# Attention block and SwiGLU on one core: tiles 4 to 7 transposed by DMA, and phi rows placed behind the next third product

## The chip, the cores and the metric

The kernel runs on one core of one Trainium2 chip. The metric is device time in microseconds (us) of one execution; the time of a kernel is the median of its runs. A core has five engines with instruction streams of their own that meet only at semaphores: PE (TensorE, matrix products into PSUM), DVE (VectorE), ACT (ScalarE), POOL (GpSimd) and SP (SyncE, which here only issues DMAs). "PEld" in the profile is the loading of PE's stationary operand, which overlaps its products.

## What is computed

The input x has 2048 tokens of width 1024. Its layer-normalized form xn feeds a linear attention of 32 heads of width 32 and a SwiGLU feed-forward of width 3584; the output joins them.

```python
xn = _layernorm(x)                        # (x - mean) / sqrt(var + 1e-5)
qkv = xn @ wqkv                           # q, k, v of 32 heads
phi = lambda t: where(t > 0, t + 1, exp(t)) + 1e-6
kv = einsum("bhsd,bhse->bhde", phi(k), v) # sums over all tokens
z = einsum("bhsd->bhd", phi(k))
o = (phi(q) @ kv) / (phi(q) . z + 1e-6)
s = o @ wo
g = silu((silu(xn @ w_gate) * (xn @ w_up)) @ w_down)
return x + s * g
```

## The kernel before

Tokens are cut into 16 tiles of 128 and into 4 blocks of 512 (block b holds tiles 4b to 4b+3; TPB = 4 tiles to a block); two blocks make a "pass" p, and `xnT[p]` holds xn transposed (features on partitions) for pass p, which is what every product needs. The matrix products of the later parts use Strassen's scheme with seven block products instead of eight: a group has part_a (products M3 and M4), part_b (M1, then M5 and M2) and part_c (N7 and N6), and each product needs sums of operand blocks that DVE forms. The stages, in order:

1. **Front** (to about 140 us; lines 264 to 755). Tile by tile: statistics, 1/sqrt, normalization, transposition, and the K and V products of tiles 0 to 8 and 12 directly; K, V and Q of the rest by Strassen groups (`KVGroup`, `QGroup`).
2. **Attention output** (to about 220 us; lines 757 to 886): KVZ, the last Q groups, numerator and denominator (ND), o written to DRAM and transposed back by DMA, times wo.
3. **Feed-forward** (the rest, lines 894 to 1230): gate and up products, h to DRAM, down product, output.

The front is written in a fixed order: inside `tc.manual_schedule(engines=FRONT_ORDER | {ET.SP})` PE, DVE, ACT, POOL and SP each run their instructions in the order in which the program emits them. An instruction that waits holds up everything behind it on its engine; on SP this includes the DMAs behind it. The names that the change touches:

- `emit_stats(i)` (L335, L348): two statistics instructions and an aggregation on DVE for tile i.
- `emit_rstd(i)` (L367 to L378): 1/sqrt for the tiles of one entry of `GROUPS`, which share one tile of results; three small instructions on DVE, then three Newton rounds of four small instructions on POOL (for block 3 these run on DVE). Before, tiles 0 to 3 are each their own group, {4, 5} and {6, 7} are groups, and blocks 2 and 3.
- `emit_N(i)` (L383): DVE normalizes tile i into its slot in the buffer `ws_all`. Tiles 4 to 7 have slots of their own; block 2's four slots are the same bytes, block 3's are others.
- `emit_T(i)` (L409, L425, L426): eight 128x128 PE transposes of tile i into two PSUM tiles, one copied to `xnT` by DVE, the other by ACT. Used for tiles 0 to 7.
- `emit_xT_block(b)` (L429, L430): for blocks 2 and 3, SP writes the block's normalized rows to `xn_dram` (1 MB), waits for that write, and issues one DMA transpose from there into `xnT`.
- `emit_B(i, c)` (L446 and the evictions L186, L187, L464): product of tile i with column chunk c of wk (c = 0, 1) or wv (c = 2, 3), eight matmuls of 512 columns; ACT takes exp and relu of K (then `emit_phi`, L190 and L191 on DVE, turns them into phi) or copies V. `emit_B_mm` and `emit_B_out` are its two halves.
- `emit_C(i)` (L475): PE adds phi(k) times v of tile i to the sums kvz; it needs phi of tile i and both V copies.
- `load_x`, `load_wkv`, and the Q weights (L315, two DMAs of 1 MB): loads issued by SP ahead of the fixed order; the Q weights wait by a gate (L755) for the first product of tile 3.
- `later`, `put` and `fill(n)`: a queue of DVE work that is put between the products by hand. In its order: statistics of block 2, its 1/sqrt, statistics of block 3, norms of block 2 and its `emit_xT_block`, 1/sqrt and norms of block 3 and its `emit_xT_block`, then the operand sums: `xs` of pass 0 (L138; the first of five reads block 0, the second block 1), sums of Q weights (L152 to L155), `xs` of pass 1 (the first reads block 2, the others block 3 too), and sums of K and V weights (L501 to L504).
- At the end of the front, `seq` runs eleven Strassen groups. Each iteration does part_a of a group, then part_c of the group before and its `post()` (for a Q or a K group two phi rows on DVE, four instructions), then its own part_b (whose first product is added to `qu` by DVE, L241 or L551), and then the C of tiles that have both phi(k) and v.

Of the kernel before, what the change touches and what calls it, by code (L numbers as in the profile page):

```python
# [21 lines left out]
def kernel(  # L22
# [11 lines left out]
    nc = tc.nc  # L34
    P = 128
# [12 lines left out]
    TPB = TB // P  # L48
# [215 lines left out]
    with ExitStack() as p1:  # L264
# [47 lines left out]
            load_wkv(c)  # L312
        for i in range(nx, NT):
            load_x(i)
        wq_loads = [nc.sync.dma_start(out=wq_sb[:, :, c * CW:(c + 1) * CW], in_=wqkv_v[:, :, c * CW:(c + 1) * CW])  # L315
                    for c in range(NCC)]

        SCH = min(nc.vector.BN_STATS_FMAX, D)
        NSC = D // SCH
# [3 lines left out]
        part_stats = {}  # L323


        GROUPS = [[t] for t in range(TPB)] + [[t, t + 1] for t in range(TPB, 2 * TPB, 2)]
        GROUPS += [list(range(b * TPB, (b + 1) * TPB)) for b in range(2, NB)]
        grp_of = {i: k for k, tiles in enumerate(GROUPS) for i in tiles}

        def emit_stats(i, parts=None):  # L330
            if i not in part_stats:
                part_stats[i] = small.tile([P, NSC, nc.vector.BN_STATS_DIM], FP32, name="stats", tag="stats")
            xr = x_ap(i).rearrange("p (c f) -> p c f", f=SCH)
            for c in (range(NSC) if parts is None else parts):
                nc.vector.bn_stats(out=part_stats[i][:, c, :], in_=xr[:, c, :])  # L335
            if parts is None:
                emit_aggr(i)
# [60 lines left out]
        def emit_N(i):  # L398
            emit_norm(i, xn_slot(i))

        def emit_T(i):

            h = DC // 2
            dst = xn_tok_ap(i)
            xn = xn_slot(i)

            def tr(t_ps, dcs):
                for k, dc in enumerate(dcs):
                    nc.tensor.transpose(t_ps[:, k, :], xn[:, dc * P:(dc + 1) * P], ident[:])  # L409

            if i == 0:
                tr_a = psB.tile([P, h, P], FP16, name="tr_ps", tag="B")[:]
                tr_b = psB.tile([P, h, P], FP16, name="tr_ps", tag="B")[:]
                emit_norm(i, xn[:, 0:h * P], cols=slice(0, h * P))
                tr(tr_a, range(0, h))
                emit_norm(i, xn[:, h * P:D], cols=slice(h * P, D))
                tr(tr_b, range(h, DC))
                nc.scalar.copy(out=dst[:, 0:h, :], in_=tr_a)  # L418
                nc.scalar.copy(out=dst[:, h:DC, :], in_=tr_b)
            else:  # L420
                tr_a = psB.tile([P, h, P], FP16, name="tr_ps", tag="B")
                tr_b = psB.tile([P, h, P], FP16, name="tr_ps", tag="B")
                tr(tr_a, range(0, h))
                tr(tr_b, range(h, DC))
                nc.vector.tensor_copy(out=dst[:, 0:h, :], in_=tr_a[:])  # L425
                nc.scalar.copy(out=dst[:, h:DC, :], in_=tr_b[:])  # L426

        def emit_xT_block(b):
            nc.sync.dma_start(out=blk_rows_pt(xn_dram, b), in_=xn_blk_slot(b))  # L429
# [22 lines left out]
        def emit_B_out(i, c):  # L452
            kv_ps = kv_tiles.pop((i, c))
            if c < NCC:
                if c == 0:
                    er_tiles[i] = exp_tile()
                    pk_tiles[i] = work.tile([P, D], BF16, name="pk_sb", tag="pk_sb")
                cs = slice(c * CW, (c + 1) * CW)
                emit_exp_relu(er_tiles[i][:, cs], pk_tiles[i][:, cs], kv_ps[:])
                if c == NCC - 1:  # L460
                    emit_phi(pk_tiles[i][:], er_tiles.pop(i)[:])
            else:
                vc = c - NCC
                nc.scalar.copy(out=v_of(i)[:, vc * GPC:(vc + 1) * GPC, 0:P],  # L464
                               in_=kv_ps[:].rearrange("p (g c) -> p g c", c=P))
# [126 lines left out]
        def fill(n):  # L592
            credit[0] += n
            while later and credit[0] > 0:
                weight, op = later.popleft()
                credit[0] -= weight
                op()
# [34 lines left out]
        with tc.manual_schedule(engines=FRONT_ORDER | {ET.SP}):  # L632

            warm_up(14)
            emit_stats(0, parts=(0,))
            emit_stats(0, parts=(1,))
            emit_aggr(0)
            emit_rstd_act(0)
            emit_T(0)
            emit_stats(1)  # L640
            warm_up(2)
            emit_B_mm(0, 0)
            emit_rstd_act(1)
            nc.scalar.preload_act_table(ACT.Exp)
            emit_N(1)
            emit_T(1)
            ln(2)
            emit_B_mm(1, 0)
            emit_B_out(0, 0)
            emit_B_mm(0, 1)  # L650
            emit_B_out(1, 0)
            emit_B_mm(1, 1)
            ln(3)
            emit_N(2)
            emit_B_out(0, 1)
            emit_B_mm(0, 2)
            emit_T(2)
            emit_B_out(1, 1)
            emit_B_mm(1, 2)
            emit_B_out(0, 2)  # L660
            emit_N(3)
            emit_B_mm(2, 0)
            emit_B_out(1, 2)
            emit_B_mm(2, 1)
            emit_stats(TPB)
            emit_T(3)
            emit_stats(TPB + 1)
            emit_rstd(TPB)
            emit_B_out(2, 0)
            emit_B_mm(2, 2)  # L670
            emit_B_out(2, 1)
            emit_stats(TPB + 2)
            emit_B_mm(0, 3)
            emit_B_out(2, 2)
            emit_B_mm(1, 3)
            emit_B_out(0, 3)
            emit_stats(TPB + 3)
            emit_rstd(TPB + 2)
            emit_C(0)
            emit_B_mm(2, 3)  # L680
            emit_B_out(1, 3)
            emit_N(TPB)
            emit_N(TPB + 1)
            emit_C(1)
            emit_B_mm(3, 0)
            emit_B_out(2, 3)
            emit_C(2)
            emit_B_out(3, 0)
            emit_B_mm(3, 1)
            fill(4)  # L690
            emit_T(TPB)
            emit_B_out(3, 1)
            emit_N(TPB + 2)
            emit_N(TPB + 3)
            emit_B_mm(3, 2)
            emit_T(TPB + 1)
            emit_B_out(3, 2)
            fill(2)
            emit_B(3, 3)
            fill(2)  # L700

            rest = list(range(TPB, 2 * TPB)) + [b * TPB for b in range(2, NB)]
            fills = {TPB: (3, 2, 2, 3), 2 * TPB: (5, 3, 2, 2), rest[-1]: (3, 4, 2, 2)}
            before = TPB - 1
            for i in rest:
                nf = fills.get(i, (3, 3, 2, 2))
                grp = QGroup(0, 0) if i == rest[-1] else None
                emit_B(i, 0)
                fill(nf[0])
                emit_C(before)  # L710
                before = i
                if grp:
                    grp.part_a()
                emit_B(i, 1)
                fill(nf[1])
                if grp:
                    grp.part_b()
                if i == TPB:
                    emit_T(TPB + 2)
                emit_B(i, 2)  # L720
                fill(nf[2])
                if i == TPB:
                    emit_T(TPB + 3)
                if grp:
                    grp.part_c()
                emit_B(i, 3)
                if grp:
                    grp.post()
                fill(nf[3])

            K, V = (lambda t: KVGroup(0, t)), (lambda t: KVGroup(1, t))
            Q = QGroup
            seq = [(lambda: Q(0, 1), 1, 0), (lambda: K(1), 1, 0), (lambda: Q(0, 2), 1, 1), (lambda: V(1), 2, 2),
                   (lambda: K(2), 0, 0), (lambda: V(2), 2, 1), (lambda: Q(0, 3), 0, 0), (lambda: K(3), 0, 0),
                   (lambda: Q(NPASS - 1, 0), 0, 0), (lambda: V(3), 0, 0), (lambda: Q(NPASS - 1, 1), 0, 0)]
            prev = None
            for make, fa, fb in seq:
                grp = make()
                grp.part_a()
                fill(fa)  # L740
                if prev:
                    prev.part_c()
                    prev.post()
                else:
                    emit_C(before)
                if make is not seq[-1][0]:
                    grp.part_b()
                    fill(fb)
                while ready_C:
                    emit_C(ready_C.popleft(), last=(not ready_C and make is seq[-1][0]))  # L750
                prev = grp
            qa = prev
            assert not later
        gate([x_loads[i] for i in range(first_wave, NT)], marks[("B", 1)], sync=True)
        gate(wq_loads, marks[("B", 3)], sync=True)  # L755

    with ExitStack() as p2:
        wop = p2.enter_context(tc.tile_pool(name="wop", bufs=1, reuse_waits="tile"))
# [502 lines left out]
```

## Time and profile before

| | |
|---|---|
| median of 3 runs | 752.52 us (751.88 to 752.78) |
| the profiled execution: time | 752.22 us |
| the profiled execution: span of its instructions | 750.4 us |
| granted TensorE clock | 1.00 throughout |
| PE transposes L409 | 64 (8 for each of tiles 0 to 7), from 6.5 to 45.8 us |
| DVE busy from 40 to 120 us | 18.4, 18.1, 17.2 and 17.4 of each 20 us |
| DMA engines idle | 26 to 32 us and 40 to 52 us |

A profile line in time order reads: start, duration, engine, line, operation, what it writes and reads, shape, count; in square brackets the idle time of the engine just before it and what ended that. "PEq", "SPq" and "ACTq" are the sequencers, SPq lines are DMA issues: the duration is how long SP is held by the issue, not how long the transfer takes. Where several alike instructions follow each other they are merged into one line with a count. Matmuls are pipelined and their printed ends are modelled, so two neighbours on PE overlap; the distance of their starts is what one costs.

### The profile page before, as it was taken

How to read it: one execution, taken by the hardware profiler on the slowest of the kernel's cores; microseconds unless marked ns; L12 is line 12 of the kernel's file. 1: busy time of each engine (PE TensorE's matmuls, PEld its weight loads, DVE VectorE, ACT ScalarE, POOL GpSimd, SP SyncE). 2: the span in 40 equal slices, each digit the busy share in tenths (PEclk: the TensorE clock that was granted, in tenths of full speed). 3: DMA queues.
4: the chain of work that ended last, by engine and by line, in shares of the span. 5: the costliest groups of instructions: out<-in, count | busy, mean ns of one | idle time of the engine just before them, and what ended most of it. 6: DMA issues, size and time to landing. Idle time of an engine off the chain costs nothing.

```text
span 750.4 us, 9920 instructions
## 1 busy us (share of the span) xinstructions
PE 741.2 (99%) x3700; PEld 350.0 (47%) x3740; DVE 510.0 (68%) x943; ACT 274.9 (37%) x482; POOL 51.6 (7%) x101
## 2 busy tenths in 40 slices
PE   9999999999999999999999999999999999999997
PEld 4554444454544444444444444444444444444454
DVE  6798977687754767886778767876755754445454
ACT  4444565655324434334343434333442111111111
POOL 3310000000000000000000000000000221121220
PEclk9999999999999999999999999999999999999999
DMA  9627000225689543665346633545879755554300
GB/s 317 219 81 169 1 1 0 71 81 130 191 235 301 151 111 99 197 183 145 105 130 179 207 113 93 173 148 150 275 242 332 297 183 183 182 183 160 106 29 29
DMA packets 127664, 115.99 MB, mean 155 GB/s; under 512 B 29440, under 2 KB 108416, under 8 KB 126336
## 3 DMA queue, kind: packets, MB, share of 16 engines
q1 hardware_dynamic: 122720, 106.58, 46.2%
q10 hardware_dynamic: 4896, 8.78, 3.4%
q8 instruction: 29, 0.48, 0.3%
q14 instruction: 19, 0.16, 0.1%
HBM read 70.52 MB, written 38.54 MB: 145 GB/s over the span
## 4 chain that ended last, share of the span: by engine, by line
PE 95%; DVE 2%; ACT 1%; issue 1%; DVEq 0%
PE X L131 29%; PE Y L131 29%; PE Z L131 10%; PE kv_ps L446 8%; PE s_ps L828 7%; PE qY L131 2%; PE qX L131 2%; PE kY L131 2%; PE kX L131 2%; PE nd_ps L791 1%; PE kvz L475 1%; PE w_ps L484 1%; PE qZ L131 1%; PE kZ L131 1%; PE tr_ps L409 0%
## 5 line engine op out<-in xcount | busy, mean ns | idle before, releaser
L131 PEld LDWEIGHTS <-ws_all 128*128 128x128 bf16 x1420 | 137.6, 98 | 162.1 <-issue 0.7
L924 DVE TENSOR_TENSOR q<-n,Y 128x512 f32<-128x512 f32 x63 | 43.3, 687 | 108.2 <-PE Y L131 105.1
L131 PEld LDWEIGHTS <-xs 128*128 128x128 bf16 (+1 forms) x736 | 69.6, 98 | 77.8 <-issue 1.4
L1194 POOL TENSOR_TENSOR o_out<-y,xres 128x512 bf16<-128x512 f32 x29 | 35.2, 1212 | 664.2 <-DVE y L1193 664.2
L131 PE MATMUL Y<-xs,ws_all 128*128 128x512 f16 (+3 forms) x308 | 70.3, 360 | 0.0
L131 PE MATMUL X<-xnT,ws_all 128*128 128x512 f16 (+1 forms) x278 | 70.1, 379 | 0.2
L131 PE MATMUL X<-xs,ws_all 128*128 128x512 f16 x224 | 57.5, 379 | 0.0
L131 PE MATMUL Z<-xs,ws_all 128*128 128x512 f16 x224 | 57.5, 379 | 0.0
L131 PE MATMUL Y<-xnT,ws_all 128*128 128x512 f16 x224 | 57.5, 379 | 0.0
L1048 ACT ACTIVATE g<-cg 128x512 bf16<-128x512 f32 x56 | 35.3, 630 | 54.1 <-DVE cg L939 54.1
L930 DVE TENSOR_TENSOR u<-Z,q 128x512 f32<-128x512 f32 x63 | 43.1, 685 | 16.0 <-PE Z L131 15.9
L1048 ACT ACTIVATE g<-X 128x512 bf16<-128x512 f32 x28 | 16.7, 597 | 99.5 <-PE X L131 99.5
L920 ACT COPY n<-X 128x512 f32<-128x512 f32 x63 | 36.9, 585 | 27.7 <-PE X L131 27.7
L446 PEld LDWEIGHTS <-xnT 128*128 128x128 f16 x320 | 30.5, 98 | 35.0 <-ACT xnT L418 0.5
L1073 DVE TENSOR_TENSOR ho<-g,up 128x1024 bf16<-128x1024 bf16 x56 | 38.1, 684 | 0.5
L446 PE MATMUL kv_ps<-wk_sb,xnT 128*128 128x512 bf16 x156 | 36.9, 379 | 0.5 <-DVE xnT L425 0.3
L1193 DVE TENSOR_TENSOR y<-y,s_in 128x512 f32<-128x512 f32 x31 | 22.2, 716 | 21.5 <-ACT y L1187 15.8
L446 PE MATMUL kv_ps<-wv_sb,xnT 128*128 128x512 bf16 x155 | 36.4, 379 | 0.2
L131 PEld LDWEIGHTS <-wg_sb 128*128 128x128 bf16 x224 | 21.9, 98 | 26.4
L131 PEld LDWEIGHTS <-wu_sb 128*128 128x128 bf16 x224 | 21.9, 98 | 26.4
L832 ACT CAST s_sb<-s_ps 128x512 bf16<-128x512 f32 x32 | 18.4, 584 | 37.9 <-PE s_ps L828 33.0
L1187 ACT ACTIVATE y<-X 128x512 f32<-128x512 f32 x8 | 4.8, 597 | 69.7 <-PE X L131 61.2
(179 smaller groups left out, 1140.6 us busy)
## 6 DMA issues: line engine op xcount, KB each, us to landing
h_dram<-ho SPq DMA_DIRECT2D x56, 256.0 KB, 2.6
wg_sb<-in_B_w_gate_dram SPq DMA_DIRECT2D x14, 512.0 KB, 4.0
wu_sb<-in_B_w_up_dram SPq DMA_DIRECT2D x14, 512.0 KB, 4.6
wdr<-in_B_w_down_dram SPq DMA_DIRECT2D x14, 512.0 KB, 4.3
ws_all<-h_dram SPq DMA_DIRECT2D x4, 1792.0 KB, 9.6
wds_dram<-wdsA SPq DMA_DIRECT2D x14, 384.0 KB, 2.8
hp_a<-h_dram SPq DMA_DIRECT2D x3, 1792.0 KB, 8.9
o_dram<-o_sb ACTq DMA_DIRECT2D x16, 256.0 KB, 2.9
```

What stands on the lines that cost most here:

```text
L131: marks["mm"] = nc.tensor.matmul(acc[:, 0:c1 - c0], lhsT=lhs(k), rhs=rhs(k)[:, c0:c1], start=(first and k == 0), stop=(k == n - 1), skip_g ...
L446: mm = nc.tensor.matmul(kv_ps[:], lhsT=xn_tok_ap(i)[:, dc, :], rhs=wkv_ap(c)[:, dc, :], start=(dc == 0), stop=(dc == DC - 1))
L475: nc.tensor.matmul(kvz_ps[j][:, gi, 0:P + 1], lhsT=pk_sb[:, g * P:(g + 1) * P], rhs=v_sb[:, g, 0:P + 1], start=(i == 0 and gi == 0), stop= ...
L828: mm = nc.tensor.matmul(s_ps[:], lhsT=oT[:, c, ttok], rhs=wo_sb[:, c, cc * CW:(cc + 1) * CW], start=(c == 0), stop=(c == G - 1))
L832: nc.scalar.copy(out=s_sb[:, cc * CW:(cc + 1) * CW], in_=s_ps[:])
L920: nc.scalar.copy(out=n[:], in_=self.X[:])
L924: nc.vector.tensor_tensor(out=self.q[:], in0=n[:], in1=self.Y[:], op=ALU.add)
L930: nc.vector.tensor_tensor(out=self.u[:], in0=Z[:], in1=self.q[:], op=ALU.add)
L1048: nc.scalar.activation(out=self.g[:, i, j * TB:(j + 1) * TB], in_=src, func=ACT.Silu)
L1073: nc.vector.tensor_tensor(out=self.ho[:, i], in0=self.g[:, i], in1=self.up[:, i], op=ALU.mult)
L1193: nc.vector.tensor_tensor(out=t[:], in0=t[:], in1=self.s_in[:, i, cs], op=ALU.mult)
L1194: (nc.vector if last and (i, j) != (0, 0) else nc.gpsimd).tensor_tensor(out=self.o_out[:, i, cs], in0=t[:], in1=self.xres[:, i, cs], op=AL ...
```

## The change

`GROUPS` becomes {0}, {1}, {2}, {3}, {4}, {5, 6, 7} and blocks 2 and 3. Tile 4's 1/sqrt is started right behind its statistics, ahead of the transposition of tile 3. `emit_T` isn't called for tiles 4 to 7 any more; in its place a new function, `emit_NT(i)`, normalizes a tile, writes its 256 KB of rows to `xn_dram` and transposes them by DMA into `xnT`, with both DMAs on SP and the second waiting for the first. Tile 4 goes there behind the phi of tile 2, tiles 5 to 7 together behind the product B(3,1). The two loads of the Q weights lose their gate and are issued by SP behind these, that is ahead of block 2's write. In the loop over `seq`, `post()` of the group before moves from ahead of part_b to behind it; the work of the `fill` after it stays behind both.

```diff
--- before.py
+++ after.py
@@ -312,8 +312,10 @@
             load_wkv(c)
         for i in range(nx, NT):
             load_x(i)
-        wq_loads = [nc.sync.dma_start(out=wq_sb[:, :, c * CW:(c + 1) * CW], in_=wqkv_v[:, :, c * CW:(c + 1) * CW])
-                    for c in range(NCC)]
+
+        def load_wq():
+            for c in range(NCC):
+                nc.sync.dma_start(out=wq_sb[:, :, c * CW:(c + 1) * CW], in_=wqkv_v[:, :, c * CW:(c + 1) * CW])
 
         SCH = min(nc.vector.BN_STATS_FMAX, D)
         NSC = D // SCH
@@ -323,7 +325,7 @@
         part_stats = {}
 
 
-        GROUPS = [[t] for t in range(TPB)] + [[t, t + 1] for t in range(TPB, 2 * TPB, 2)]
+        GROUPS = [[t] for t in range(TPB + 1)] + [list(range(TPB + 1, 2 * TPB))]
         GROUPS += [list(range(b * TPB, (b + 1) * TPB)) for b in range(2, NB)]
         grp_of = {i: k for k, tiles in enumerate(GROUPS) for i in tiles}
 
@@ -424,6 +426,13 @@
                 tr(tr_b, range(h, DC))
                 nc.vector.tensor_copy(out=dst[:, 0:h, :], in_=tr_a[:])
                 nc.scalar.copy(out=dst[:, h:DC, :], in_=tr_b[:])
+
+        def emit_NT(i):
+
+            emit_N(i)
+            rows = xn_dram[i * P:(i + 1) * P, :]
+            nc.sync.dma_start(out=rows, in_=xn_slot(i))
+            nc.sync.dma_start_transpose(out=xn_tok_ap(i), in_=rows)
 
         def emit_xT_block(b):
             nc.sync.dma_start(out=blk_rows_pt(xn_dram, b), in_=xn_blk_slot(b))
@@ -663,24 +672,23 @@
             emit_B_out(1, 2)
             emit_B_mm(2, 1)
             emit_stats(TPB)
+            emit_rstd(TPB)
             emit_T(3)
             emit_stats(TPB + 1)
-            emit_rstd(TPB)
             emit_B_out(2, 0)
             emit_B_mm(2, 2)
             emit_B_out(2, 1)
+            emit_NT(TPB)
             emit_stats(TPB + 2)
             emit_B_mm(0, 3)
             emit_B_out(2, 2)
             emit_B_mm(1, 3)
             emit_B_out(0, 3)
             emit_stats(TPB + 3)
-            emit_rstd(TPB + 2)
+            emit_rstd(TPB + 3)
             emit_C(0)
             emit_B_mm(2, 3)
             emit_B_out(1, 3)
-            emit_N(TPB)
-            emit_N(TPB + 1)
             emit_C(1)
             emit_B_mm(3, 0)
             emit_B_out(2, 3)
@@ -688,12 +696,11 @@
             emit_B_out(3, 0)
             emit_B_mm(3, 1)
             fill(4)
-            emit_T(TPB)
+            for i in range(TPB + 1, 2 * TPB):
+                emit_NT(i)
+            load_wq()
             emit_B_out(3, 1)
-            emit_N(TPB + 2)
-            emit_N(TPB + 3)
             emit_B_mm(3, 2)
-            emit_T(TPB + 1)
             emit_B_out(3, 2)
             fill(2)
             emit_B(3, 3)
@@ -715,12 +722,8 @@
                 fill(nf[1])
                 if grp:
                     grp.part_b()
-                if i == TPB:
-                    emit_T(TPB + 2)
                 emit_B(i, 2)
                 fill(nf[2])
-                if i == TPB:
-                    emit_T(TPB + 3)
                 if grp:
                     grp.part_c()
                 emit_B(i, 3)
@@ -740,19 +743,19 @@
                 fill(fa)
                 if prev:
                     prev.part_c()
-                    prev.post()
                 else:
                     emit_C(before)
                 if make is not seq[-1][0]:
                     grp.part_b()
-                    fill(fb)
+                if prev:
+                    prev.post()
+                fill(fb)
                 while ready_C:
                     emit_C(ready_C.popleft(), last=(not ready_C and make is seq[-1][0]))
                 prev = grp
             qa = prev
             assert not later
         gate([x_loads[i] for i in range(first_wave, NT)], marks[("B", 1)], sync=True)
-        gate(wq_loads, marks[("B", 3)], sync=True)
 
     with ExitStack() as p2:
         wop = p2.enter_context(tc.tile_pool(name="wop", bufs=1, reuse_waits="tile"))
```

## The prediction

> **What bounds the kernel now.** I read the engine table first, then PE's waits, then PE, DVE and the DMA queue of SP in order of time around the changed lines.
>
> ```profile
> PE 741.2 (99%) x3700; PEld 350.0 (47%) x3740; DVE 510.0 (68%) x943; ACT 274.9 (37%) x482; POOL 51.6 (7%) x101
> ```
> PE is busy for 741.2 of 750.4 us: only PE work removed, or one of its few stalls, can shorten the run. From 80 to 125 us its waits are these:
> ```profile
> PE kX L131 <- ACT v_sb L537: 0.6, 1, 0.6
> PE kvz L475 <- ACT v_sb L464: 0.3, 1, 0.3
> ```
> The PE timeline prices a PE transpose of a tile:
> ```profile
> 34.96 0.61 PE L409 MATMUL tr_ps<-ident,ws_all 128*128 128x128 f16 x8
> 35.41 1.67 PE L446 MATMUL kv_ps<-wv_sb,xnT 128*128 128x512 bf16 x7
> 37.13 0.61 PE L409 MATMUL tr_ps<-ident,ws_all 128*128 128x128 f16 x8
> 37.58 1.89 PE L446 MATMUL kv_ps<-wv_sb,xnT 128*128 128x512 bf16 x8
> ```
> The printed 0.61 overlaps what follows; start to start it is 0.45 us. A product of eight matmuls takes 1.73 us the same way.
>
> The DVE timeline after 70 us holds a second limit close under PE:
> ```profile
> 70.13 1.22 DVE L138 TENSOR_TENSOR xs<-xnT 128x2048 f16<-128x2048 f16 x1
> 72.56 3.50 DVE L138 TENSOR_TENSOR xs<-xnT 128x2048 f16<-128x2048 f16 x3 [1.22 <-DMA xnT<-xn_dram]
> ...
> 89.73 0.68 DVE L251 TENSOR_TENSOR pqT<-qu,qY 128x512 bf16<-128x512 f32 x1
> ```
> DVE waits 1.22 us for the transposed block 3 at 72.56, and then runs to L251 at 89.73 with no idle in brackets. L251 releases ACT (exp, relu, exp, relu, then the V copy L464), and PE waits for that copy:
> ```profile
> 92.84 0.39 PE L475 MATMUL kvz<-v_sb,pk_sb 128*128 128x129 bf16 x4 [0.27 <-ACT v_sb L464]
> ```
> So PE at 92.84 is tied to **block 3's landing** at 72.56, 20.3 us before. That landing ends a serial chain on SP:
> ```profile
> 31.45 1.00 SPq L315 DMA_DIRECT2D wq_sb<-in_A_wqkv_dram  x2
> 51.97 0.39 SPq L429 DMA_DIRECT2D xn_dram<-ws_all  x1
> 56.34 5.51 SPq L430 DMA_TRANSPOSE xnT<-xn_dram  x1
> 61.94 0.53 SPq L429 DMA_DIRECT2D xn_dram<-ws_all  x1
> 66.64 3.87 SPq L430 DMA_TRANSPOSE xnT<-xn_dram  x1
> ```
> Write block 2, wait for it (4.4 us), transpose it (SP is held 5.5), write block 3 (4.7), transpose it (lands 5.9 after issue). The Q weights went out at 31.45, in a hole of this queue.
>
> **The change, part by part.**
>
> PE: four transposes (tiles 4 to 7) go, 4 x 0.45 = **-1.8 us** of PE work, all before 46 us. Off the path, DVE loses four copies L425 (0.37 to 0.42 each), ACT four of 0.58.
>
> Tile 4's own 1/sqrt: the number of chains stays (one for {4}, one for {5,6,7}, where it was {4,5} and {6,7}). The three small DVE operations move ahead of the copy of T(3), where DVE idles 1.00 us: nothing; without that idle 0.6 us.
>
> Tile 4: its normalization follows the phi that ends at 26.8, so its write goes out at about 27.3. Uncontended, such a 256 KB write leads to its transpose 2.1 to 2.35 us later (o_dram issued 163.14 and 167.41, transposes 165.44 and 169.53), and that lands 3.1 to 4.4 after issue (median 3.3): about 33. PE wants it at 39.31 less two transposes, 38.4. Covered by 5 us.
>
> Tiles 5 to 7: statistics take 1.45 us a tile, so DVE reaches their 1/sqrt at 27.3 + 2.9 = 30.2, its preparation ends at 30.8, POOL's chain took 3.6 to 4.0 (I take 3.8): 34.6. Norm 5 ends at 35.2. On SP each tile is a write, a wait, and a transpose that holds SP 1.25 us (row L815: 1232 to 1298 ns). The first wait is 2.25; the next two writes stand behind a transpose's data, for which the o_dram row gives a landing of 2.1 to 3.8; I take 2.9, its median. Transposes at 37.45, 41.6 and 45.75 us, SP free at 47.0; tiles land by 41, 45 and 49. PE wants them at 47.57, 54.94 and 62.30, less 1.8. Covered by 4.8 us and more, so PE doesn't stall here.
>
> The Q weights now go out at 47.0 instead of 31.45. Their first reader is L152 at 65.36, so they themselves are not late. What they are **moved in front of** is block 2's write. Their 2 MB kept the DMA engines busy from about 32.8 to 38.9 us (shares 0.61, 1.09, 1.09, 0.50 in the 2 us windows from 32): 6.1 us. Behind the last tile's data (45.75 + 3 = 48.75) they end at 54.85. DVE comes to block 2's norms earlier: from 35.2, two norms 1.0, phi 1.2, two statistics 2.9, small operations 0.6, a statistic 1.45, a wait for ACT to 43.1, phi 1.2, three statistics 4.35, four norms 1.9: 50.6, where it was 51.94. The write is issued at 50.65 and its data (2.8 us: shares 0.56 and 0.85 from 52 to 56) move from 54.85 to 57.65; 0.6 later it has landed, 58.3 against 56.34. From there I keep the measured steps: 5.6 to the write of block 3, 4.7 to its transpose, 5.9 to landing: **74.5 instead of 72.5, +2.0 us**. DVE has done its earlier work by 70 and idles there. PE, 1.8 us ahead until then, first meets C(8): phi(8) ended at 77.2, is at 79.2 now, and PE would be there at 77.0. It meets the rest at C(12): 92.84 + 2.0. So the transposes' saving is lost in that wait, and the term is +2.0, not -1.8 + 2.0.
>
> Bounds: shortest writes (2.2 each), both block transposes at 3.87: weights from 47.4 to 53.5, block 2 landed at 56.8, block 3's write at 60.8, landing 71.4, or **-1.2**. Writes of 3.8 (the o_dram row's longest): weights end at 57.4, block 2 at 61, then 5.6 + 5.0 + 5.9 = 77.5, or **+4.9**.
>
> Is the write really behind the weights? An x tile of 256 KB, issued behind 1 MB weights, landed after 7.6 us (median), against 2.9 for o_dram. That shows sharing or strict order, not which. The Trainium skill ("DMA: Bandwidth & Descriptors", section Queues, rings and completion order) says that each engine consumes one ring's descriptors in order; the row agrees, and by that rule the sum is as above. By sharing, about 1.4 MB of weights and the 1 MB write would move together at 350 GB/s, the write would land 1.3 us earlier, and the term would be +0.7.
>
> Phi rows behind the next group's third product: the same DVE instructions, in another order. In the old order phi of K(1) (107.04 to 109.5) stood ahead of L241 at 109.50, and its two rows waited 0.23 and 0.15 us for ACT. With L241 ahead those waits are filled: about 0.25 us earlier at L251 (113.05), which feeds the one PE stall of this stage (0.74 us start to start: 115.16 to 116.76 less 0.86). Other stalls (103.63, 104.60, 109.88, 110.85; 0.5 us in all) hang on ACT's copies and stay. Bounds: 0 and -0.74, as the new wait is for PE's third product, which is there before. I take **-0.25**. Phi of a K group is wanted an iteration later, so no C waits for it.
>
> After 122 us PE runs without a stall up to the KVZ stage, and everything later follows PE, so a shift at 93 us stays to the end.
>
> Sum: +2.0 - 0.25 = **+1.75 us**. The profiled execution took 752.22 us, 750.4 of it span, 1.8 around it: 754.0. The median of the runs is 752.52, 0.3 above: **754.3 us**.
>
> **Rivals.**
> (a) The delay is mostly covered: the rings share, or block 2's transpose holds SP less than 5.5 (the other took 3.87, which alone gives +0.4). Term +0.7 - 0.25: 752.9. For it: two such transposes differ by 1.6 us with nothing in the page to say why. Chance 0.22.
> (b) **Faster**: the queue keeps its pace. If block 3 lands before 71.3 (72.56 less 1.25), the DVE stretch starts earlier and PE keeps up to 1.8 us; with the lower bound, -1.2, and phi between -0.25 and -0.74, about -1.65: 750.9. For it: DVE is 1.3 us early at block 2's norms, and without the weights in front block 3 would land at 71.2. Against it: the weights' 6.1 us of data must then end by 53.5. Chance 0.23.
> (c) Every write behind a transpose takes 3.8: 752.5 + 4.9 - 0.25 = 757.2. Chance 0.05.
> That the change doesn't do what it says I exclude: the calls that put the transposes of tiles 4 to 7 on PE are deleted.
> The forecast has 0.50.
>
> **How the numbers follow.** A measurement of this kernel can tell about 0.2%, 1.5 us, from no change. Case (b) is faster: 0.23. Case (a): same, 0.22. The forecast is 0.25 us over the slower bound (754.03); its own spread goes to both sides, but much of the lower half is counted in (a), so with (c) slower is 0.55. The forecast's own range is 753 to 756 (queue term +0.8 to +3.7); reaching to most of (b), and leaving out (c), 750.5 to 756.5.
>
> **What would show it.** L409 falls from 64 to 32 matmuls, and B(4,3), tile 4's last product, starts about 1.8 us earlier. On SP: transposes near 30, 37.5, 41.6 and 45.8, the Q weights near 47, block 2's write near 50.7 but its transpose only near 58. On DVE: the wait at the second xs of block 3 grows from 1.2 to about 5 us. On PE: new waits at C(8) (about 2) and C(12), and the v_sb L537 wait shrinks below 0.57. I am wrong if block 2's transpose goes out before 57 us, if block 3 lands before 72.5, or if PE passes C(12) without a wait.

## The result and the profile after

The kernel after takes **756.01 us** (median of 6 runs, 754.88 to 758.09); the kernel before took 752.55 (751.88 to 753.22) beside it. The ratio is 1.0049, interval [1.0034, 1.0064]: 3.5 us slower, where the forecast was 1.75 us slower. That is about twice the forecast's change, and the time lies at the upper edge of its own range of 753 to 756. The profiled execution is the longest of the six: 758.09 us, span 756.3 (the other spans are 753.1 to 754.8). Its excess over the span before, 5.9 us, is therefore not the excess of the median, and the experiments below are needed to read it.

The engine table of the page after:

```profile
PE 742.8 (98%) x3669; PEld 348.5 (46%) x3708; DVE 508.8 (67%) x939; ACT 273.1 (36%) x478; POOL 49.8 (7%) x101
```

PE has 31 recorded matmuls fewer (the four transposes were 32), yet is busy 1.6 us longer. Part of that is a lower clock for a few us, shown in the last section. The DMA queue of SP, in the view by time (start, duration, what). The block write and its transposes are now L438 and L439:

```profile
47.16 1.20 SPq L318 DMA_DIRECT2D wq_sb<-in_A_wqkv_dram  x2
51.78 0.38 SPq L438 DMA_DIRECT2D xn_dram<-ws_all  x1
60.06 3.93 SPq L439 DMA_TRANSPOSE xnT<-xn_dram  x1
64.04 0.58 SPq L438 DMA_DIRECT2D xn_dram<-ws_all  x1
69.86 4.43 SPq L439 DMA_TRANSPOSE xnT<-xn_dram  x1
```

From block 2's write to its transpose it is 8.28 us where it was 4.37. DVE then waits for block 3 at its second xs, and PE for DVE, in the views of DVE and PE by time:

```profile
76.42 3.50 DVE L138 TENSOR_TENSOR xs<-xnT 128x2048 f16<-128x2048 f16 x3 [5.50 <-DMA xnT<-xn_dram]
```

```profile
81.14 0.64 PE L484 MATMUL kvz<-v_sb,pk_sb 128*128 128x129 bf16 x8 [2.66 <-DVE pk_sb L191]
...
96.91 0.39 PE L484 MATMUL kvz<-v_sb,pk_sb 128*128 128x129 bf16 x4 [0.27 <-ACT v_sb L473]
...
175.24 1.90 PE L831 MATMUL s_ps<-wo_sb,oT 128*128 128x512 bf16 x7 [1.36 <-DMA oT<-o_dram]
```

The first is the wait at C(8) that the prediction named. At C(12) it named a new one; the 0.27 us there is the wait that the kernel before had too, only 4.07 us later. The v_sb wait behind it (now L546) has not shrunk either: 0.6, as before. The third, far behind the change, is new: there PE waited for nothing before. From C(12) to the first s_ps product it is 78.33 us where it was 76.64: 1.69 more. With the 4.07, together 5.76 of the 5.9.

### The profile page after: what moved, and what is told of

The parts are those of the page before. It is cut to its first block, busy times and chain, and to the rows that moved or that the text cites. A ratio compares the mean times of both kernels' runs of the same rounds, so it can differ in the third digit from the quotient of the medians.

```text
span 756.3 us, 9865 instructions
## 1 busy us (share of the span) xinstructions
PE 742.8 (98%) x3669; PEld 348.5 (46%) x3708; DVE 508.8 (67%) x939; ACT 273.1 (36%) x478; POOL 49.8 (7%) x101
## 4 chain that ended last, share of the span: by engine, by line
PE 86%; DMA 5%; DVE 4%; ACT 3%; SPq 1%; issue 1%; DVEq 0%
PE X L131 29%; PE Y L131 28%; PE Z L131 10%; PE s_ps L831 7%; PE kv_ps L455 4%; DMA xn_dram<-ws_all 2%; PE qY L131 2%; DMA wv_sb<-in_A_wqkv_dram 2%; PE qX L131 2%; PE kY L131 1%; PE kX L131 1%; ACT e_t L186 1%; PE nd_ps L794 1%; DMA xnT<-xn_dram 1%; ACT pqT L187 1%
## 5 line engine op out<-in xcount | busy, mean ns | idle before, releaser
L831 PE MATMUL s_ps<-wo_sb,oT 128*128 128x512 bf16 x123 | 29.0, 379 | 1.6 <-DMA oT<-o_dram 1.4
```

The lines of the kernel that those rows point to most:

```text
L831: mm = nc.tensor.matmul(s_ps[:], lhsT=oT[:, c, ttok], rhs=wo_sb[:, c, cc * CW:(cc + 1) * CW], start=(c == 0), stop=(c == G - 1))
```

## The experiments

Each kernel ran on one chip with the kernel before beside it, whose median was 752.32 for the first four and the last two, 752.28 for the others. A table of all first, then each one. "C(12)" is the start of its second half in the profile; "o write" is the first o_dram write, "gap" the time from it to its transpose, "load" the start of the nearest transfer of queue q8 (below), all in us. From the first s_ps product to the end of the span it is 580.9 to 581.4 us in all twelve profiles: what is lost or won ahead of it stays.

| kernel | median us | ratio, interval | C(12) | o write | load | gap | wait at s_ps |
|---|---|---|---|---|---|---|---|
| before | 752.5 | 1 | 92.84 | 163.14 | 158.6 | 2.30 | none |
| after | 756.01 | 1.0049 [1.0034, 1.0064] | 96.91 | 166.94 | 167.9 | 3.95 | 1.36 |
| e1_wq_early | 751.76 | 0.9989 [0.998, 0.9998] | 90.69 | 160.72 | 162.7 | 4.58 | 1.19 |
| e2_phi_only | 752.32 | 1.0001 [0.9992, 1.001] | 92.79 | 163.08 | 158.7 | 2.59 | none |
| e3_no_phi | 755.41 | 1.004 [1.0028, 1.0053] | 94.51 | 164.53 | 165.5 | 4.51 | 0.99 |
| e4_wq_half | 751.84 | 0.9993 [0.9984, 1.0001] | 90.97 | 160.99 | 161.9 | 3.77 | 0.94 |
| e5_early_shift | **750.8** | 0.998 [0.997, 0.9989] | 91.33 | 161.36 | 156.9 | 3.13 | none |
| e6_early_actw_shift | 751.12 | 0.998 [0.9971, 0.9989] | 92.30 | 162.32 | 158.4 | 2.82 | none |
| e7_before_actwrite | 752.72 | 1.0003 [0.9994, 1.0012] | 92.91 | 162.93 | 158.7 | 2.19 | none |
| e8_after_shift | 752.86 | 1.0008 [0.9999, 1.0016] | 92.99 | 163.01 | 158.6 | 3.08 | none |
| e9_before_shift | 754.3 | 1.0023 [1.0014, 1.0032] | 93.46 | 163.77 | 164.4 | 3.42 | 1.08 |
| e10_after_shift2 | 754.11 | 1.0023 [1.0014, 1.0032] | 94.59 | 164.61 | 156.8 | 3.14 | none |

### The weights out of the way of block 2: e1 and e4

e1 is the kernel after with the Q weights behind tile 4 instead of behind tile 7:

```
             emit_NT(TPB)
+            load_wq()
...
-            load_wq()
```

> The changed kernel with one thing altered: the Q weights are issued behind tile 4's DMA transpose (about 32 us) instead of behind tile 7's (47 us), so nothing stands between the tiles and block 2's write. Theory Q (block 3 lands late because 2 MB of weights stand ahead of block 2's write, and PE is tied to that landing): block 2's write goes out near 51, its transpose near 55.5, block 3 lands at 71 to 72.5 us, the DVE wait at the second xs of pass 1 falls from 5.5 to 1 to 2.5 us, time 751 to 752.5 us, that is 3.5 to 5 us below the changed kernel and 0 to 1.5 below the one before. Rival D (the four round trips by tile, holding SP, are what costs): the time stays near 756. Rival J (the moved phi rows cost it): stays near 756.

e4 leaves one half of them (1 MB) at its place and puts the other behind block 3's transpose:

```
-        def load_wq():
-            for c in range(NCC):
+        def load_wq(cs=(0,)):
+            for c in cs:
...
         put_norms(NB - 1)
+        put(0, [lambda: load_wq((1,))])
```

> The changed kernel with only one of the two 1 MB halves of the Q weights ahead of block 2's write; the other is issued behind block 3's transpose (about 71 us; its first reader is L152 for the third column group, near 86 us). Theory Q: 1 MB less is 3.0 us less of data ahead of block 2's write, so block 2's transpose near 57 instead of 60, block 3 at 73 to 74, time 752.5 to 753.5 us: half way. Rival D: near 756.

The SP queue of e1 by time:

```profile
30.50 1.19 SPq L318 DMA_DIRECT2D wq_sb<-in_A_wqkv_dram  x2
...
50.09 0.39 SPq L438 DMA_DIRECT2D xn_dram<-ws_all  x1
54.52 4.08 SPq L439 DMA_TRANSPOSE xnT<-xn_dram  x1
58.66 0.57 SPq L438 DMA_DIRECT2D xn_dram<-ws_all  x1
63.31 3.89 SPq L439 DMA_TRANSPOSE xnT<-xn_dram  x1
```

and that of e4:

```profile
45.50 0.57 SPq L318 DMA_DIRECT2D wq_sb<-in_A_wqkv_dram  x1
50.37 0.38 SPq L438 DMA_DIRECT2D xn_dram<-ws_all  x1
54.73 3.94 SPq L439 DMA_TRANSPOSE xnT<-xn_dram  x1
```

Without the 2 MB right ahead of it, block 2's write leads to its transpose in 4.43 us again (after: 8.28), and one megabyte issued 4.9 us before it costs it nothing (4.36). So e4 did not come out half way, as expected, and the cost isn't spread evenly over the weights: it begins with what has not drained when the write is issued. C(12) comes 2.15 (e1) and 1.87 us (e4) earlier than before. The profiles differ in when their first K product starts (7.58 us before, 7.23 in e1, 7.51 in e4); counted from there C(12) is 1.80 us earlier in both. That is the saving of the PE transposes, which the prediction priced at 1.8: it arrives whole once block 3 is there. But the run gains only 0.6 and 0.5 us, because both then wait at s_ps:

```profile
168.69 1.90 PE L831 MATMUL s_ps<-wo_sb,oT 128*128 128x512 bf16 x7 [1.19 <-DMA oT<-o_dram]
```

(e1, PE by time.) Neither the weights nor the transposes touch that place. This gap between 2.15 and 0.6 led to the second half of the study.

### The order of phi and L241: e2 and e3

e2 is the kernel before with the moved post() alone; e3 the kernel after with the old order:

```
                 if prev:
                     prev.part_c()
-                    prev.post()
                 else:
                     emit_C(before)
                 if make is not seq[-1][0]:
                     grp.part_b()
-                    fill(fb)
+                if prev:
+                    prev.post()
+                fill(fb)
```

> The kernel before with only the phi rows moved behind the next third product. The prediction had -0.25 us (752.3). The trace of the changed kernel says 0: the DVE time gained ahead of L555 is given back in a new wait of 0.36 us for ACT's copy, and PE's stall of 0.57 at the V group stays: 752.5. Rival J (the moved rows cost 2 us or more): 754.5 or above.

> The changed kernel with the phi rows back in their old place, so only the transposes, the 1/sqrt and the Q weights are changed. Theory Q: 756 (755.5 to 756.5), the same as the changed kernel. Rival J: 752 to 753.

e2 is worth nothing, 1.0001 [0.9992, 1.001], and after and e3 (1.0049 and 1.004, intervals overlapping) can't be told apart. DVE by time in e2:

```profile
111.25 0.69 DVE L546 TENSOR_TENSOR qu<-qu,kY 128x512 f32<-128x512 f32 x1 [0.36 <-ACT qu L543]
...
112.99 0.68 DVE L251 TENSOR_TENSOR pqT<-qu,qX 128x512 bf16<-128x512 f32 x1
```

L546 now waits 0.36 us for ACT's copy of qu, and L251 starts at 112.99 against 113.05 before. DVE arrives earlier, and the time goes into a wait on ACT. PE's stall behind it is 0.57 us in e2 as in before.

### Where the instruction loads fall: e8, e5, e9 and e10

The page counts 29 transfers "q8 instruction" with 0.48 MB, that is 16 KB each. PE and PEld have 3669 + 3708 = 7377 records: 7377/256 = 28.8. Their starts are about as far apart as 256 of PE's instructions, and e9 below, with 3796 + 3836 records (29.8 times 256), has 30. I take them for the loads of PE's program; the trace doesn't name the engine. The Trainium skill ("Runtime: NRT & Kernel Launch", section Instruction fetch mechanics) says that an engine's instructions come in blocks of 16 KiB, 256 instructions, over its own DMA queue, and calls the cost "mostly hidden". The counts agree. Hidden it is for PE, which shows no stall at a load; whether for others, the next lines ask. They are the DMA view of the 4 us around the first o_dram write, in 40 slices: busy tenths of the 16 DMA engines, and GB/s. First before, from 163 us, then after, from 166.8:

```profile
DMA  0000000301889999720000000000000000000047
GB/s 0 0 0 0 0 0 0 82 0 61 307 328 369 389 389 430 266 62 21 0 0 0 0 0 0 0 0 0 0 0 0 0 0 0 0 0 0 23 97 166
...
q14 instruction: 1, 0.01, 0.8%
```

```profile
DMA  0000000004987889822001000101010001000000
GB/s 0 0 0 0 0 0 0 0 0 102 512 328 287 328 328 389 287 41 82 20 20 41 20 0 0 20 0 20 0 20 20 20 20 41 0 0 0 0 0 0
...
q8 instruction: 1, 0.02, 2.3%
q14 instruction: 2, 0.02, 1.6%
```

The body of the write is as quick in both, 0.7 us at about 270 to 510 GB/s. After, a tail of mostly 20 to 40 GB/s with gaps follows for 1.6 us; 20 is about a sixteenth of the body's rate, as if one of the 16 engines were still moving its share. A load of q8 lies in this window and none in before's. The change took 64 instructions from PE (32 matmuls and 32 weight loads), so every later load moved by a quarter of its period, and one came to lie on this write.

A second queue of instruction loads, q14 (19 transfers, 0.16 MB in the page, so 8 KB each), has to be held apart from q8. Its loads start 0.6 to 1.8 us after this write is issued in every kernel but e7: one in before, e2 and e9, two in the other eight. They come with a tail too, as in e8 from 163 us, where no load of q8 lies:

```profile
GB/s 0 0 0 0 0 0 0 0 143 287 369 307 553 369 307 205 123 0 20 0 20 20 20 20 21 0 0 0 0 0 0 0 0 0 0 0 0 0 0 0
...
q14 instruction: 2, 0.02, 1.0%
```

The gap from the write to its transpose goes up with both. It is 2.19 us with no load (e7), 2.30 and 2.59 with one of q14 alone, 2.82 to 3.14 with two; 3.42 with one and a load of q8 (e9), 3.77 to 4.58 with two and a load of q8. PE waits at s_ps only in the last two groups. So the loads of q14, which are in nearly all kernels, do not make the wait by themselves; the one of q8 comes on top.

The test moves the loads of q8 and leaves the work of the later stages alone. The warm-up at the start has 14 matmuls of 512 columns; with more and narrower ones it has about as many columns and more instructions:

```
-        def warm_up(n):
+        def warm_up(n, cols=TB):
             for _ in range(n):
-                nc.tensor.matmul(w_ps[:], lhsT=warm[:, 0:P], rhs=warm[:], start=True, stop=True)
+                nc.tensor.matmul(w_ps[:, 0:cols], lhsT=warm[:, 0:P], rhs=warm[:, 0:cols], start=True, stop=True)
...
-            warm_up(14)
+            warm_up(46, 156)
```

These are 64 more instructions, which bring the loads back to where they lay before. e8 is the kernel after with this edit, e5 is e1 with it.

> The changed kernel with the same shift of PE's instructions as e5. Theory L: the wait for oT (1.0 to 1.4 us) goes; block 3's write loses the load that made it 1.1 us longer, block 2's transpose gets one (+1.5), so block 3 lands 0.4 later: time 755 to 755.4 against 756.0. Rival T: 756.

> e1 (Q weights behind tile 4) with the first warm-up on PE cut into 46 matmuls of 156 columns instead of 14 of 512: the same columns, 64 PE instructions more, so that PE has as many instructions ahead of the later stages as the kernel before, and its 16 KB instruction loads (queue q8, every 256 PE instructions) fall where they fell there. Theory L (the instruction load that falls on the first write of o_dram makes that write land late, and PE waits for its transpose): the load moves from 162.7 to about 157 to 158 us, the first transpose of o_dram follows its write by 2.1 to 2.6 us instead of 4.6, PE's wait for oT (1.2) is gone. The same shift puts a load back into block 2's transpose, which holds SP 5.5 again instead of 4.1, and takes back some 0.5 us at C(12). Time 751.0 (750.5 to 751.5). Rival T (the DMA transposes by tile make later DMAs slow, wherever the loads fall): the wait for oT stays near 1.2 and the time is 751.7 or more.

e9 goes the other way: the kernel before, with its work unchanged, and 192 more (110 matmuls of 65 columns), which puts the loads where the change put them. e10 is the kernel after with 128 more (78 of 92).

> The kernel before with nothing changed but its warm-up: 110 matmuls of 65 columns instead of 14 of 512, that is 192 PE instructions more and about the same number of columns. 192 more shift the 256-instruction loads as 64 fewer do, so that a load should fall where it falls in the kernel after: near 162 us, on the first o_dram write, and near 63 us, on block 3's write. Theory (where the instruction loads fall decides): this alone makes the kernel slower by 0.8 to 2 us, 753.1 to 754.3; the write of o_dram to its transpose takes 3.5 us or more instead of 2.3, PE waits about 1 us at s_ps for oT, and block 2's transpose holds SP about 4 us instead of 5.5. Rival (the loads are harmless; what cost time after the change was the queue alone): 752.1 to 752.7, no wait at s_ps.

> The kernel after with its warm-up as 78 matmuls of 92 columns instead of 14 of 512: 128 PE instructions more, so that the loads fall 128 instructions earlier than after the change: near 25, 49, 73, 104, 127, 150 us, on no write of blocks 2 and 3 and on none of o_dram. Theory (loads): the o_dram transpose follows its write within 2.6 to 3.2 us, no wait at s_ps, block 2's transpose holds SP about 4 us, and the time is 752 to 753.5, as with 64 more. Rival (the shape of the warm-up, or where it leaves the clock, is what 64 more instructions changed, not where a load falls): a wait at s_ps stays, 754 to 756.

e8 takes back 3.15 of the 3.5 us (752.86 against 756.01), e5 another 0.96 us of e1, and e9 makes the kernel before 1.98 us slower. The expectation for e8 was 755 to 755.4: it took the load to fall into block 2's transpose again, which it doesn't (below). PE by time at the first s_ps in e8 and in e9:

```profile
169.79 1.89 PE L831 MATMUL s_ps<-wo_sb,oT 128*128 128x512 bf16 x8
```

```profile
171.36 1.90 PE L828 MATMUL s_ps<-wo_sb,oT 128*128 128x512 bf16 x7 [1.08 <-DMA oT<-o_dram]
```

The wait goes with the load, in the kernel with the change and in the one without. In the table it stands in the five kernels whose load starts 0.6 to 2 us after the write is issued, and in none of the other seven. e9's 1.9 us of span are 0.62 at C(12), from a later start of everything (the Q weights too go out 0.62 later), and 1.26 between C(12) and s_ps. Its ten runs lie in two groups, three at 752.8 to 753.1 us and seven at 754.1 to 754.8; one profile, of the second group, can't say whether the load misses the write in the first. So, where it happens, this coincidence costs **about 1.3 us** (C(12) to s_ps is 1.26 to 1.69 longer in the five kernels), and that it does is shown. That it is the 16 KB packet itself that holds up one engine is the reading of the tail, not a test of its own.

Not all of the difference between these runs is loads. The warm-up itself takes a different time, in after and in e8 by PE:

```profile
1.19 6.16 PE L493 MATMUL w_ps<-warm 128*128 128x512 bf16 x14 [1.19 <-DVE warm L90]
```

```profile
1.19 4.85 PE L493 MATMUL w_ps<-warm 128*128 128x156 bf16 x46 [1.19 <-DVE warm L90]
```

The same 14 matmuls take 4.96 to 6.16 us in seven profiles, the 46 narrower ones 4.85 to 6.15 in three, so this is not the edit's doing alone. With it moves the first K product, to between 7.05 and 8.25 us. e9's later start is just this (8.21 against 7.58, 0.63 later), and part of e8's lead at C(12) comes from there: its first K product is 0.71 earlier than e3's and 1.15 earlier than in the profiled execution of after. The wait at s_ps is apart from it. How much of the 3.15 us and of the 1.98 the start takes in the median, one profile each can't say.

The same shift changes the block writes. Before, a load at 58.8 us lay in block 2's transpose; after, one at 65.4 lies in block 3's write. SP's queue in e8, where the load is at 57.1:

```profile
50.09 0.38 SPq L438 DMA_DIRECT2D xn_dram<-ws_all  x1
57.91 4.09 SPq L439 DMA_TRANSPOSE xnT<-xn_dram  x1
62.04 0.58 SPq L438 DMA_DIRECT2D xn_dram<-ws_all  x1
66.92 3.80 SPq L439 DMA_TRANSPOSE xnT<-xn_dram  x1
```

Block 3's write takes 4.88 us to its transpose, where after had 5.82 and e3, with a load at 63.8, 5.81. In both of these a load of q14 starts within 0.1 us of q8's, so the 5.8 are the two together; e8 has one of q14 alone on the write, and before and e2, with 4.70, have none. Block 2's transpose holds SP 3.9 to 4.1 us in after, e1, e3, e4, e8, e9 and e10, and 5.1 to 5.8 in before, e2, e5, e6 and e7, where the load of q8 falls in it. That answers why the two transposes before differed, 5.51 and 3.87.

e10 didn't come out as expected: 754.11, not 752 to 753.5. The wait at s_ps is gone, as expected, and block 3's write takes 4.87 us. What remains is an early delay, in PE by time:

```profile
16.45 1.90 PE L455 MATMUL kv_ps<-wv_sb,xnT 128*128 128x512 bf16 x8 [1.09 <-DMA wv_sb<-in_A_wqkv_dram]
```

Block 2's write is issued at 51.50 us, 1.41 later than in e8, and C(12) comes 1.60 later. Of the 1.41, the first K product has 0.20 (7.30 against 7.10); the rest is the wait for wv. A load at 10.6 us lies in the loading of wv, but after's profiled execution also ran late there (first tile written at 28.56 us, e3 27.62, e8 26.86) with its load at 21.7. So what makes wv late stays open, and that loads alone set the time is not shown for the stage before 50 us.

### The write of block 3 from another engine: e6 and e7

Would block 3 land earlier if its write didn't stand behind block 2's transpose on SP? e7 is the kernel before, e6 is e5, with

```
-            nc.sync.dma_start(out=blk_rows_pt(xn_dram, b), in_=xn_blk_slot(b))
+            (nc.scalar if b == NB - 1 else nc.sync).dma_start(out=blk_rows_pt(xn_dram, b), in_=xn_blk_slot(b))
```

> e5 with block 3's write issued by ACT instead of SP, so that it lands while block 2's transpose holds SP. If block 3's landing is still a limit in e5, it comes 3 us earlier here and C(12) is at 90.7 or earlier: time 750.5 (750.0 to 751.0). If DVE's own work is the limit from here on, it is the same as e5.

> The kernel before with block 3's write issued by ACT: block 3 lands about 3 us earlier, and DVE's wait of 1.2 us for it goes. PE still has its 32 transposes. Theory Q says that PE's own work is only 0.3 us behind DVE there, so the gain is 0.3 (752.0): neither the earlier landing nor the removed transposes bring 2 us alone, only both. Rival (the landing alone is worth it): 750.5 to 751.

Both are worth nothing: e7 has the time of before, e6 the ratio of e5. The DMA queues of ACT and SP in e7:

```profile
58.46 0.40 ACTq L429 DMA_DIRECT2D xn_dram<-ws_all  x1
```

```profile
66.67 3.93 SPq L430 DMA_TRANSPOSE xnT<-xn_dram  x1
```

The write goes out 3.5 us earlier than before (61.94) and its transpose at the same time (66.64 before): 8.2 us instead of 4.7. So block 3 did not land 3 us earlier, as both expectations had it, and neither run says what an earlier landing alone is worth. In e7 no packet of ACT's queue (q10) moved from 58.5 to 63 us, while the data of block 2's transpose did; all 528 of them (1.05 MB) moved from 63 to 67. What the write got is the engines' time behind that data, not an earlier place. The Trainium skill ("DMA: Bandwidth & Descriptors", section Issuing engines are not separate DMA queues) says that DMAs from different engines run on the same 16 and interleave, and that starting them from several saves only the time of issuing. The last agrees here; an interleaving these rows don't show.

## Why the prediction came out as it did

**The direction and the first half of the mechanism held.** The transposes' 1.8 us are real (1.80 in e1 and e4, counted from the first K product) and were lost in a wait for block 3, whose chain on SP was lengthened by the weights ahead of block 2's write. The wait at C(8) is where the prediction put it, with 2.66 us for its 2. That write took 8.28 us to its transpose (7.65 forecast), and 7.7 to 8.0 in e3, e8 and e10; with the weights elsewhere 4.4. The rival in which the delay is mostly covered allows C(12) at most 0.7 late, that is 93.54; the one in which the queue keeps its pace has it earlier than before. After and e3 have 96.91 and 94.51. With the loads shifted, though, e8 has 92.99 and a time of 752.86: there the first of these rivals (752.9) would have been the better forecast, for the reason that it gave, a transpose of block 2 that holds SP 4 us and not 5.5.

**The queue term, +2.0,** was measured as +1.67 at C(12) in e3 (+1.44 counted from the first K product), whose total (755.41) is nearest to the median of after. The profiled execution of after has +4.07, of which 0.94 is its later first tile against e3. So the size was about right, but in part by luck, by steps whose errors stand against each other: "I keep the measured steps: 5.6 to the write of block 3, 4.7 to its transpose". After, they were 3.98 and 5.82. The 5.6 was no property of a block's transpose: a load lay in it, and the change moved that load to the next write. Of the 1.52 us that C(12) lies earlier in e8 than in e3, 0.93 are block 3's write (4.88 and 5.81) and 0.58 the earlier issue of block 2's write.

**That PE at C(12) is tied to block 3's landing** was read too strongly out of the kernel before. In e9, which has the same work behind the warm-up, DVE doesn't wait for block 3 at all:

```profile
70.75 4.62 DVE L138 TENSOR_TENSOR xs<-xnT 128x2048 f16<-128x2048 f16 x4
```

Yet the 0.27 us at C(12) is there, and from the first K product to C(12) it is 85.25 us, as before (85.26). PE's own work set C(12); the landing stood just behind it. In the six kernels where PE came to wait longer at C(12) (e2, e3, e5, e6, e8, e10) C(12) lies 20.17 us after the second xs, and before it lay 20.28 after it, 0.11 more. With so little room a later landing moves C(12) nearly one for one, so the sum did not suffer; but an earlier landing alone, as e7 was to bring, could have gained nothing there.

**The term that failed is the sentence "After 122 us PE runs without a stall up to the KVZ stage, and everything later follows PE, so a shift at 93 us stays to the end".** The shift did not stay: between C(12) and s_ps it grew by 1.31 us in e3 (77.95 against 76.64) and by 1.69 in after, where PE came to wait for oT. No term was given to the 64 instructions that PE no longer has. Only the work in them was counted, not that all loads behind them shift.

**Phi, -0.25,** was 0 (e2). The bound of nothing was the right end: DVE's next step depended on ACT.

In sum, for e3: 1.67 + 1.31 = 2.98 against a measured 3.09. The forecast had 2.0 and -0.25 in their place.

Of the change's parts, the transposes by DMA are a gain where the weights don't stand in front of the block's write. **e5**, with both causes removed, is faster than both kernels, though by little: 750.8 us, 0.998 [0.997, 0.9989] of before.

## What to carry to other kernels

When a change adds or removes many instructions of an engine, look where its instruction loads fall before and after (a queue of the DMA table, with a time in the windows): a load that lies on a short write with a waiting transpose behind it can cost most of what the edit saves (e1: 1.8 us won at C(12), 0.6 left), and a few narrower warm-up matmuls move it. When a large load is moved, ask which write is issued next, and whether the load has drained by then. A duration that differs between two equal DMAs is not to be carried over into a sum until it is known why.

## What the runs showed of the hardware

**A transpose's data stopped where an instruction load fell.** The DMA view from 56 to 62 us of before, 40 slices:

```profile
DMA  0020000000006878899999990001000059999999
GB/s 0 0 55 0 0 0 0 0 0 0 0 20 155 184 162 140 138 237 387 254 268 212 56 9 0 0 0 9 9 9 10 9 128 285 297 292 285 292 292 287
```

The data of block 2's transpose start at 57.7, all but stop from 59.5 to 60.8, and go on at 285 to 297 GB/s. The load took from 58.8 to 60.1, so the halt begins and ends some 0.7 us behind it. In after, where none lies there until 65.4, the same data run from 61.4 to 65 without a break. The halt, 1.3 us, is most of the 1.6 that SP was held longer; why the transpose's issue should wait for a load of another engine no run here shows.

**The clock fell after a stall of 2.66 us.** Four windows of 1 us of after (busy us by engine, then PE's granted clock, DMA share and GB/s):

```profile
82.00:83.00 1.00, 1.00 (x4) 0.34 (x3) 1.00 (x2) 0.14 (x1) 0.00 (x0) 0.66 0.00 0
83.00:84.00 1.00, 1.00 (x4) 0.39 (x3) 1.00 (x2) 0.45 (x1) 0.00 (x0) 0.50 0.00 0
84.00:85.00 1.00, 1.00 (x4) 0.34 (x3) 1.00 (x2) 0.00 (x0) 0.00 (x0) 0.50 0.00 0
85.00:86.00 1.00, 1.00 (x4) 0.39 (x3) 1.00 (x2) 0.00 (x0) 0.00 (x0) 0.63 0.00 0
```

e3, with a stall of 1.69 us at the same place, kept 1.00. It cost about 0.3 us at C(12), since DVE was the later one: from the second xs to C(12) it is 20.49 us in after and 20.17 in e3. The Trainium skill ("TensorE: Matmul & The Clock Gate", section Part 1: The HAM clock gate) gives half rate after an idle window of about 3.4 us; the half agrees, but here a shorter stall brought it, seen in one execution.
